# Linear attention followed by a routed mixture of experts: 64x64 score tiles, state before the scores, and a new order of the stores, gathers and first turned rows

## The chip, the cores and the metric

The kernel runs on one core of a Trainium2 chip. The metric is the device time of one execution in microseconds (us); the number shown for a kernel is the median of its runs. One execution was also taken by the hardware profiler, and all lines of a profile below come from that one execution. Engines are named as the profile names them: PE is TensorE (PEld its weight load), DVE is VectorE, ACT is ScalarE, POOL is GpSimd, SP is SyncE, which here issues nearly all plain DMAs (SPq is its queue). L573 is line 573 of the kernel.

## The reference

The input is q, k, v and f_logit of shape 4 x 8 x 768 x 48 (batch, heads, positions, head dimension), all fp32. The first part is a recurrence over the positions of each head:

```python
f = 1.0 / (1.0 + np.exp(-f_logit))
for t in range(S):
    state = f[:, :, t, :, None] * state + np.einsum('bhd,bhe->bhde', k[:, :, t], v[:, :, t])
    y[:, :, t] = np.einsum('bhd,bhde->bhe', q[:, :, t], state)
```

Its result becomes x, 3072 rows of 384. The second part routes every row to two of eight experts by noisy logits, and adds up their weighted results:

```python
noisy_logits = x @ w_gate + np.log1p(np.exp(x @ w_noise)) * noise
top2 = np.argpartition(-noisy_logits, 2, axis=1)[:, :2]      # weights: softmax over the two
h = np.maximum(x[mask] @ w1[e], 0.0)                         # w1: 384 x 1024
out[mask] += top2_w[mask, k, None] * (h @ w2[e])             # w2: 1024 x 384
```

## The kernel before

The recurrence is worked in chunks of 128 positions. There are 24 chunks, n = c * 4 + b: block c of six along the sequence, batch b of four. Each chunk covers all eight heads, two heads (a pair hp, with halves par 0 and 1 in partitions 0 to 63 and 64 to 127) side by side in 128 partitions, each head padded from 48 to 64. With L the running sum of the logarithms of the forget gates, the chunk needs P = exp(-L) and Q = exp(L); q times P is called qP and k times Q is called kQ (`scaled`). The stages of a chunk are:

- `forget` turns f on PE (fp, L533) and makes its logarithm on ACT. `summed` is a scan on DVE (L547). `decays` makes P, Q and `far`, a copy of the last column of L, on ACT (L552, L554, L555).
- `scaled` turns q and k on PE (qp and kp, L533) and multiplies them on DVE into qP and kQ (L559, L561), reading PSUM.
- `scores` turns kQ back on PE into kn (L567), where n // 4 < 5, and multiplies kQ and qP of every head, 128 x 128, into sc (L573). Eight heads fill two banks of PSUM. DVE multiplies them by the causal mask, 0 or 1, into A (L576).
- `output` adds v times A (L591) and, where c > 0, state times qP (L602) in the same banks y; between them stands ds, the product of kn and v (L597). ACT copies y out (L606) and ds out (L611); POOL makes the next state (L615, L618, L619).
- `features` multiplies y by a matrix that brings it back to rows and gives the logits of the router too (xp, L626). DVE adds the logits up (L629), ACT copies the rows, xs (L631), and a store of xs to x_rows in DRAM is put on the list xw.

A matmul's tile of the array follows from its operands: 64 contracted rows and 128 columns of the stationary operand are written 64*128 in the profile, and so on.

The loop runs over i, and a step i takes one stage each of different chunks: in steady state forget of chunk i+3, scaled of i+1, scores of i, summed of i+2, output of i-1, decays of i+2, features of i-2. A last call ties every engine's instructions to the order in which the program wrote them, so each engine's order is that of the loop, and no instruction overtakes another on its engine.

Loads are written after the stage of the same step: f after forget, q and k for three chunks ahead after scaled, v after scores. All go through SP; so do the stores of x_rows, taken from the list xw after scaled (L632), parts of the first experts' weights (L834, L837) and the clearing of `out`. Buffers of f, q, k and v are rings of 5, 4, 4 and 6 chunks.

Routing of a block c starts after its four chunks: `route` makes the entries and their slots, and POOL writes them into lists in DRAM by indirect DMA (L703, "puts", at most one in every second or third slot of the loop). When the first three blocks are routed, `first_loads` begins for the first 256 rows of experts 0 to 3: `fetch` reads a piece of the list by SP (slots, L808), `gather` reads the rows that it names by POOL's indirect DMA (xg, L819), and `turned` turns them on PE (xgp, L855) and copies them. `first_loads` is moved on by one at each slot of the loop, seven slots per step, and waits by counting slots. Its order of acts and pauses is a table of its own. Once "turned" is done, `pieces`, the products of the experts, are written between the last stages of the attention (hp, L907).

After the attention come the experts' products, from about 153 us to the end. They aren't changed.

## Time and profile before

| | |
|---|---|
| median of 3 runs | 655.39 us (652.59 to 659.07) |
| the profiled execution's own time | 659.87 us |
| its span, first to last instruction | 658.1 us |
| mean granted clock of TensorE | 0.987 |
| PE busy | 637.8 us (97%) |
| PEld, DVE busy | 551.1 us (84%), 442.8 us (67%) |
| ACT, POOL busy | 254.1 us (39%), 270.2 us (41%) |
| DMA, mean bandwidth | 145 GB/s, 96.31 MB |
| packets under 512 B | 115600 of 153897 |
| sc, L573, 384 records | 64*128, mean 291 ns |
| y, L602, 320 records | 64*64, mean 286 ns |

A record is one entry of the profile. A duration of a matmul's record includes its way through the array, so records of one engine overlap; the time that a block of matmuls costs is read from the start of its first record to the start of the next block. A group's "idle" is the time for which the engine had stood still before it, and what ended that is named behind an arrow. In the chain of waits each piece of time is put down to what the end of the execution waited for. The windows give the busy time of every engine in a stretch, then the granted clock, the share of time in which the 16 DMA engines were busy, and GB/s.

### The profile page before, as it was taken

The numbers are of one execution on the slowest core, as the hardware profiler recorded it, in microseconds if no ns is written. First come the engines' busy times: TensorE is split into PE (matmuls) and PEld (weight loads), VectorE is DVE, ScalarE is ACT, GpSimd is POOL, SyncE is SP. The second block draws the span as 40 slices with busy tenths as digits, with TensorE's granted clock in tenths as the row PEclk, the third lists the DMA queues.
The fourth block names the chain that finished last, engine by engine and source line by source line (L and its number), as shares of the span: only waits on it lengthen the run. The fifth ranks groups of instructions, "written<-read, shape, count | busy, mean of one in ns | idle before, by whom it ended". The sixth has DMA issues, their size and how long they took to land.

```text
span 658.1 us, 12894 instructions
## 1 busy us (share of the span) xinstructions
PE 637.8 (97%) x4883; PEld 551.1 (84%) x4883; DVE 442.8 (67%) x993; ACT 254.1 (39%) x602; POOL 270.2 (41%) x301
## 2 busy tenths in 40 slices
PE   8999999979999999999999999999999999999991
PEld 8999999868989999989758965995698579899891
DVE  6777877954566577677657575666666666766751
ACT  6876776642222133233332233223332332232320
POOL 7743999743188521252501450334035114413021
PEclk9999999998999999999999999999999999999996
DMA  9999898774799323368707560925275247602112
GB/s 191 193 220 205 181 191 173 179 209 110 256 348 237 64 36 86 82 192 286 195 28 245 98 192 0 316 41 176 74 242 127 63 143 191 178 2 26 21 25 29
DMA packets 153897, 96.31 MB, mean 146 GB/s; under 512 B 115600, under 2 KB 146320, under 8 KB 153824
## 3 DMA queue, kind: packets, MB, share of 16 engines
q1 hardware_dynamic: 141648, 76.12, 42.0%
q0 software_dynamic: 12176, 19.25, 15.0%
q8 instruction: 41, 0.67, 0.4%
q14 instruction: 32, 0.26, 0.1%
HBM read 75.97 MB, written 19.62 MB: 145 GB/s over the span
## 4 chain that ended last, share of the span: by engine, by line
PE 90%; DMA 5%; SPq 1%; DVE 1%; POOL 1%; issue 0%; ACT 0%; POOLq 0%; DVEq 0%
PE y L1014 31%; PE P L932 8%; PE W L932 5%; PE Z L932 5%; PE V L932 5%; PE X L932 5%; PE hp L907 5%; PE sc L573 4%; PE y L591 4%; PE xp L626 3%; PE xgp L855 2%; PE y L602 2%; PE kp L533 1%; PE ds L597 1%; PE fp L533 1%; PE qp L533 1%
## 5 line engine op out<-in xcount | busy, mean ns | idle before, releaser
L1023 POOL DMA_INDIRECT out_dram<-ys,slots x48 | 80.3, 1672 | 150.0 <-ACT ys L1084 121.9
L1014 PE MATMUL y<-qk_all,f_all 128*128 128x192 f32 x576 | 105.3, 327 | 0.5 <-DVE f_all L996 0.5
L1014 PEld LDWEIGHTS y<-qk_all,f_all 128*128 128x128 f32 x576 | 93.3, 190 | 1.1 <-DVE f_all L996 1.1
L819 POOL DMA_INDIRECT xg<-x_rows,slots x48 | 52.9, 1102 | 50.8 <-DMA slots<-lists 35.0
L1014 PE MATMUL y<-w,hs_b 128*128 128x192 f32 x320 | 59.1, 328 | 0.0
L703 POOL DMA_INDIRECT lists<-entry,sloti x48 | 54.8, 1142 | 10.3 <-issue 9.5
L1014 PEld LDWEIGHTS y<-w,hs_b 128*128 128x128 f32 x320 | 52.9, 190 | 0.9
L1158 POOL DMA_INDIRECT out_dram<-ys_q,slots_q x5 | 8.6, 1720 | 104.4 <-DVE ys_q L1156 104.4
L907 PE MATMUL hp<-xt_a,w 128*128 128x256 f32 x192 | 43.4, 382 | 0.0
L968 ACT ACTIVATE hs_b<-hs_b 128x256 f32<-128x256 f32 (+1 forms) x32 | 15.1, 470 | 71.7 <-DVE hs_b L948 71.7
L907 PEld LDWEIGHTS hp<-xt_a,w 128*128 128x128 f32 x192 | 35.9, 190 | 4.9 <-issue 0.3
L932 PE MATMUL X<-xt_a,w 128*128 128x256 f32 (+1 forms) x128 | 39.7, 432 | 0.0
L932 PE MATMUL Z<-xt_b,v_all 128*128 128x256 f32 (+1 forms) x128 | 39.7, 432 | 0.0
L1073 DVE TENSOR_TENSOR ys<-P,y 128x192 f32<-128x192 f32 x24 | 8.5, 354 | 41.6 <-PE y L1014 25.6
L948 DVE TENSOR_TENSOR hs_b<-hs_a,X 128x256 f32<-128x256 f32 (+1 forms) x32 | 15.6, 487 | 29.9 <-PE X L932 29.7
L576 DVE TENSOR_TENSOR A<-sc,causal 128x1024 f32<-128x1024 f32 x24 | 29.3, 1221 | 8.9 <-PE sc L573 8.8
L1014 PE MATMUL y<-w,f_all 128*128 128x192 f32 x192 | 35.2, 326 | 0.0
L1084 ACT ACTIVATE ys<-ys,slots 128x384 f32<-128x384 f32 x23 | 14.1, 615 | 54.1 <-DVE ys L1080 54.1
L932 PEld LDWEIGHTS X<-xt_a,w 128*128 128x128 f32 x128 | 24.3, 190 | 10.1
L932 PEld LDWEIGHTS Z<-xt_b,v_all 128*128 128x128 f32 x128 | 24.3, 190 | 10.1
L948 DVE TENSOR_TENSOR hs_a<-hs_a,P 128x256 f32<-128x256 f32 (+1 forms) x64 | 31.1, 486 | 1.4
L1014 PEld LDWEIGHTS y<-w,f_all 128*128 128x128 f32 x192 | 31.8, 190 | 0.0
(200 smaller groups left out, 1442.2 us busy)
## 6 DMA issues: line engine op xcount, KB each, us to landing
w<-in_moe_w_dram SPq DMA_DIRECT2D x16, 1536.0 KB, 8.5
w_q<-in_moe_w_dram SPq DMA_DIRECT2D x10, 1536.0 KB, 10.3
w<-in_moe_w_dram SPq DMA_DIRECT2D x16, 384.0 KB, 6.1
f_all<-in_f_logit_dram SPq DMA_DIRECT2D x24, 192.0 KB, 3.7
qk_all<-in_q_dram SPq DMA_DIRECT2D x24, 192.0 KB, 4.9
qk_all<-in_k_dram SPq DMA_DIRECT2D x24, 192.0 KB, 4.9
v_all<-in_v_dram SPq DMA_DIRECT2D x24, 192.0 KB, 4.4
x_rows<-xs SPq DMA_DIRECT2D x24, 192.0 KB, 4.4
```

Source lines behind the costliest of these rows:

```text
L533: nc.tensor.transpose(p[:, cols(hp)], flat[:, cols(hp)], ident)
L573: nc.tensor.matmul(sc[:, par, cols(hp)], lhsT=kQ[n][rows(par), cols(hp)], rhs=qP[n][rows(par), cols(hp)], start=True, stop=True)
L576: nc.vector.tensor_tensor(A[n].rearrange("j r (a i) -> j (r a) i", i=C), sc.rearrange("j r (a i) -> j (r a) i", i=C), causal.unsqueeze(1). ...
L591: nc.tensor.matmul(at(hp, par), lhsT=vt[:, 2 * hp + par, :], rhs=A[n][:, par, cols(hp)], start=(hp < 2), stop=(c == 0 and hp >= HP - 2))
L626: nc.tensor.matmul(xp[:, hp, :], lhsT=yT[n][:, hp % 2, cols(hp // 2)], rhs=w_rt[:, hp, :], start=True, stop=True)
L703: into = nc.gpsimd.indirect_dma_start(out=lists, out_offset=bass.IndirectOffsetOnAxis(ap=sloti[:, r, b:b + 1], axis=0), in_=entry[:, c, b, ...
L819: nc.gpsimd.indirect_dma_start(out=xg[p][:, s, :], out_offset=None, in_=x_rows[0:HALF * B * C] if p < NE else x_rows, in_offset=bass.Indir ...
L907: nc.tensor.matmul(hp[:, o, :], lhsT=w1[home(k)][:, i, (fo + o) * 128:(fo + o + 1) * 128], rhs=xt_a[:, i, k % 2 * 256:(k % 2 + 1) * 256], ...
L932: nc.tensor.matmul(to, lhsT=x, rhs=y, start=start, stop=stop)
L948: nc.vector.tensor_tensor(to, x, y, ALU.add)
L1014: nc.tensor.matmul(P[name], lhsT=x[:, o, :], rhs=y[:, o, :], start=(o == 0), stop=(o == FH - 1))
L1023: into = nc.gpsimd.indirect_dma_start(out=out, out_offset=bass.IndirectOffsetOnAxis(ap=slots[p][:, s, 2:3], axis=0), in_=ys[s], in_offset= ...
```

## The change

- **Scores.** The 128 x 128 scores of a head are made as 64 x 64 tiles of the array. Of the four quarters of a head (early and late keys, early and late queries), that of late keys and early queries is always zero under the mask, and isn't computed. Each head has two products: one of one half of the keys with all 128 queries, and one of the other half with the late 64 queries. PSUM for the scores (`sc_all`) is taken once and cleared once by DVE, so what is never written is zero.
- **Swapped halves.** For pairs hp 2 and 3 (heads 4 to 7) the two halves of the 128 keys are swapped in kQ, and so in kn, in the scores and in v. `scaled` therefore writes kQ by two operations; v is loaded by three DMAs, one for heads 0 to 3 and one for each half of heads 4 to 7; the mask has a plane for each pair hp.
- **State before the scores.** `from_state`, the product of state and qP, of chunk n-1 is written between kn and the scores of chunk n, and opens the accumulation in y.
- **Q and far** are made at the end of step i for chunk i+2 (`rising`), after features of that step, in place of within `decays`.
- **Stores of x_rows** are written after the stage output, so after the loads of v, in place of after scaled.
- **`first_loads`** starts two slots sooner, gathers the rows of p = 1 before the turning of p = 0, and turns p = 0 six slots after the last gather.
- **The empty list** that clears the lists has half the size and is stored twice.

```diff
@@ -422,8 +422,8 @@
         turns.append(turns.pop(0))
         return turns[-1].tile([128, 512], F32, tag="one", name=name)
 
-    def two_banks(name):
-        return ps2.tile([128, 2, 512], F32, tag="two", name=name)
+    sc_all = ps2.tile([128, 2, 512], F32, tag="two", name="sc_all")
+    nc.vector.memset(sc_all, 0.0)
 
 
     ident = const.tile([128, 128], F32, tag="ident", name="ident")
@@ -463,9 +463,12 @@
     over_of = counting("over_of", [[QS, NI]], base=3 * 256)
     block = counting("block", [[1, NI]])
 
-    causal = const.tile([128, 128], F32, tag="causal", name="causal")
-    nc.gpsimd.affine_select(out=causal, in_=ones, compare_op=ALU.is_ge, fill=0.0, base=0,
-                            pattern=[[1, 128]], channel_multiplier=-1)
+    T = C // 2
+    causal = const.tile([128, HP, 128], F32, tag="causal", name="causal")
+    for hp in range(HP):
+        for base, n in ((0, 128),) if hp < HP // 2 else ((T, 128), (-T, T)):
+            nc.gpsimd.affine_select(out=causal[0:n, hp], in_=(causal[0:n, hp] if n == T else ones), compare_op=ALU.is_ge, fill=0.0,
+                                    base=base, pattern=[[1, 128]], channel_multiplier=-1)
     earlier = const.tile([128, 128], F32, tag="earlier", name="earlier")
     nc.gpsimd.affine_select(out=earlier, in_=ones, compare_op=ALU.is_ge, fill=0.0, base=-1,
                             pattern=[[1, 128]], channel_multiplier=-1)
@@ -474,7 +477,7 @@
     LR = E * N + 256
     x_rows = tc.dram_tile([N, DM], F32, name="x_rows")
     lists = tc.dram_tile([LR, 4], U32, name="lists")
-    empty = const.tile([128, LR // 128, 4], U32, tag="empty", name="empty")
+    empty = const.tile([128, LR // 256, 4], U32, tag="empty", name="empty")
 
     cap = [const.tile([128, HP, C], F32, tag=f"cap{i}", name=f"cap{i}") for i in range(2)]
     for i in range(2):
@@ -518,8 +521,15 @@
     def load(nm, n):
         c, b = n // B, n % B
         if n < NCH * B:
-            nc.sync.dma_start(out=pads[nm][n % RING[nm]][:, :, 0:D],
-                              in_={"f": f_logit, "q": q, "k": k, "v": v}[nm][b, :, c * C:(c + 1) * C, :].rearrange("h t d -> t h d"))
+            to = pads[nm][n % RING[nm]][:, :, 0:D]
+            rows_in = {"f": f_logit, "q": q, "k": k, "v": v}[nm][b, :, c * C:(c + 1) * C, :]
+            if nm != "v":
+                nc.sync.dma_start(out=to, in_=rows_in.rearrange("h t d -> t h d"))
+                return
+            nc.sync.dma_start(out=to[:, 0:H // 2], in_=rows_in[0:H // 2].rearrange("h t d -> t h d"))
+            for half in range(2):
+                nc.sync.dma_start(out=to[half * T:(half + 1) * T, H // 2:],
+                                  in_=rows_in[H // 2:, (1 - half) * T:(2 - half) * T].rearrange("h t d -> t h d"))
 
     def clamp(n, engine=nc.gpsimd):
         if n < NCH * B:
@@ -551,14 +561,20 @@
         P[n] = wk.tile([128, HP * C], F32, tag="P", name=f"P_{n}", bufs=4)
         nc.scalar.activation(P[n], L[n], AF.Exp, scale=-1.0)
         Q[n] = wk.tile([128, HP * C], F32, tag="Q", name=f"Q_{n}")
-        nc.scalar.activation(Q[n], L[n], AF.Exp)
-        nc.scalar.copy(far[:, n, :], L[n].rearrange("d (a t) -> d a t", t=C)[:, :, C - 1])
+
+    def rising(n):
+        if 0 <= n < NS:
+            nc.scalar.activation(Q[n], L[n], AF.Exp)
+            nc.scalar.copy(far[:, n, :], L[n].rearrange("d (a t) -> d a t", t=C)[:, :, C - 1])
 
     def scaled(n):
         qP[n] = wk.tile([128, HP * C], F32, tag="qP", name=f"qP_{n}", bufs=3)
         nc.vector.tensor_tensor(qP[n], transposed("q", n), P[n], ALU.mult)
         kQ[n] = wk.tile([128, HP * C], F32, tag="kQ", name=f"kQ_{n}")
-        nc.vector.tensor_tensor(kQ[n], transposed("k", n), Q[n], ALU.mult)
+        kt = transposed("k", n)
+        for far_ in range(2):
+            out_, x, y = (z.rearrange("d (o a s t) -> d o a s t", o=2, s=2, t=T)[:, far_] for z in (kQ[n], kt, Q[n]))
+            nc.vector.tensor_tensor(out_[:, :, ::-1, :] if far_ else out_, x, y, ALU.mult)
 
     def scores(n):
         if n // B < NCH - 1:
@@ -567,40 +583,49 @@
                 nc.tensor.transpose(kp[:, cols(hp)], kQ[n][:, cols(hp)], ident)
             kn[n] = wk.tile([C, H, DP], F32, tag="kn", name=f"kn_{n}")
             nc.scalar.copy(kn[n].rearrange("t h d -> t (h d)"), kp)
-        sc = two_banks(f"sc_{n}")
-        for hp in range(HP):
-            for par in range(2):
-                nc.tensor.matmul(sc[:, par, cols(hp)], lhsT=kQ[n][rows(par), cols(hp)],
-                                 rhs=qP[n][rows(par), cols(hp)], start=True, stop=True)
+        if n:
+            from_state(n - 1)
+        for hp in (0, 2, 1, 3):
+            for late_rows in range(2):
+                half = hp // 2 ^ late_rows
+                for par in range(2):
+                    nc.tensor.matmul(sc_all[half * T:(half + 1) * T, par, hp * C + late_rows * T:(hp + 1) * C],
+                                     lhsT=kQ[n][rows(par), hp * C + half * T:hp * C + (half + 1) * T],
+                                     rhs=qP[n][rows(par), hp * C + late_rows * T:(hp + 1) * C], start=True, stop=True)
         A[n] = wk.tile([C, 2, HP * C], F32, tag="A", name=f"A_{n}")
-        nc.vector.tensor_tensor(A[n].rearrange("j r (a i) -> j (r a) i", i=C), sc.rearrange("j r (a i) -> j (r a) i", i=C),
-                                causal.unsqueeze(1).broadcast_to((C, H, C)), ALU.mult)
+        nc.vector.tensor_tensor(A[n], sc_all, causal.rearrange("j a i -> j (a i)").unsqueeze(1).broadcast_to((C, 2, HP * C)), ALU.mult)
+
+    y_of = {}
+
+    def place(n, hp, par):
+        return y_of[n][hp % 2][rows(par ^ hp % 2), cols(hp // 2)]
+
+    def from_state(n):
+        y_of[n] = [one_bank(f"y{odd}_{n}") for odd in range(2)]
+        if n // B:
+            for hp in range(HP):
+                for par in range(2):
+                    nc.tensor.matmul(place(n, hp, par), lhsT=state[n % B][rows(par), hp, :],
+                                     rhs=qP[n][rows(par), cols(hp)], start=(hp < 2), stop=False)
 
     def output(n):
         c, b = n // B, n % B
         vt = pads["v"][n % RING["v"]]
 
 
-        y = [one_bank(f"y{odd}_{n}") for odd in range(2)]
-
-        def at(hp, par):
-            return y[hp % 2][rows(par ^ hp % 2), cols(hp // 2)]
-
+        if n not in y_of:
+            from_state(n)
+        y = y_of[n]
         for hp in range(HP):
             for par in range(2):
-                nc.tensor.matmul(at(hp, par), lhsT=vt[:, 2 * hp + par, :], rhs=A[n][:, par, cols(hp)],
-                                 start=(hp < 2), stop=(c == 0 and hp >= HP - 2))
+                nc.tensor.matmul(place(n, hp, par), lhsT=vt[:, 2 * hp + par, :], rhs=A[n][:, par, cols(hp)],
+                                 start=(c == 0 and hp < 2), stop=(hp >= HP - 2))
         if c < NCH - 1:
             ds = one_bank(f"ds_{n}")
             for hp in range(HP):
                 for par in range(2):
                     nc.tensor.matmul(ds[rows(par), hp * DP:(hp + 1) * DP], lhsT=kn[n][:, 2 * hp + par, :],
                                      rhs=vt[:, 2 * hp + par, :], start=True, stop=True)
-        if c:
-            for hp in range(HP):
-                for par in range(2):
-                    nc.tensor.matmul(at(hp, par), lhsT=state[b][rows(par), hp, :],
-                                     rhs=qP[n][rows(par), cols(hp)], start=False, stop=(hp >= HP - 2))
         yT[n] = wk.tile([128, 2, HP // 2 * C], F32, tag="yT", name=f"yT_{n}")
         for odd in range(2):
             nc.scalar.copy(yT[n][:, odd, :], y[odd][:, 0:HP // 2 * C])
@@ -1258,10 +1283,10 @@
     def first_loads():
         while n_routed < HALF or len(n_put) < HALF * B * 2:
             yield
-        for _ in range(7):
+        for _ in range(5):
             yield
-        for what, p, pause in (("fetch", 1, 4), ("first", 0, 0), ("second", 0, 3), ("fetch", 2, 7), ("turned", 0, 0),
-                               ("first", 1, 3), ("second", 1, 1), ("fetch", 3, 1)):
+        for what, p, pause in (("fetch", 1, 4), ("first", 0, 0), ("second", 0, 3), ("fetch", 2, 5), ("first", 1, 1), ("second", 1, 6),
+                               ("turned", 0, 0), ("fetch", 3, 1)):
             if what == "fetch":
                 ahead(what, p)
             elif what == "first":
@@ -1311,16 +1336,17 @@
                         load(nm, n + 3)
                 if n in (1, 2):
                     load_router(n - 1)
-                while xw:
-                    xw.pop(0)()
             elif stage is scores:
                 for m in (n + 1,) if n < 4 else (2 * n - 3, 2 * n - 2) if n < 6 else (n + 3,):
                     load("v", m)
                 if n in (2, 6, 7, 8, 9, 10):
                     load_router(2 + (2, 6, 7, 8, 9, 10).index(n))
                 elif n == 5:
-                    nc.sync.dma_start(out=lists.rearrange("(p r) w -> p r w", p=128), in_=empty)
+                    for part in range(2):
+                        nc.sync.dma_start(out=lists.rearrange("(g p r) w -> g p r w", g=2, p=128)[part], in_=empty)
             elif stage is output:
+                while xw:
+                    xw.pop(0)()
                 if 9 <= n < 17:
                     part_of_weights(0, 1 + (n - 9) // 4, (n - 9) % 4)
                 elif n >= NS - 2:
@@ -1336,6 +1362,7 @@
             if done["turned"] and (n_first < 5 or i >= NS - 3 and stage is not forget) and (n_first < 11 or i >= NS - 1):
                 next(pieces)
                 n_first += 1
+        rising(i + 2)
         if i < 0:
             warm_up(4)
         if i >= NS - 1:
```

## The prediction

> **What bounds the kernel now.** I read the windows, then the order of instructions in one chunk, the chain of waits around 140 us, and SyncE's queue.
>
> Windows (busy us of PE, PEld, DVE, ACT and POOL, granted clock, DMA share, GB/s):
>
> ```profile
> 60.00:100.00 40.00, 40.00 (x592) 36.44 (x595) 32.41 (x83) 29.08 (x79) 33.15 (x46) 1.00 0.88 185
> ...
> 126.00:132.00 6.00, 6.00 (x88) 5.33 (x87) 5.86 (x13) 3.69 (x10) 2.38 (x4) 1.00 0.80 173
> ...
> 142.00:146.00 4.00, 0.00 (x0) 0.00 (x0) 0.71 (x4) 0.48 (x1) 3.26 (x6) 0.93 0.89 276
> 146.00:153.00 7.00, 6.88 (x56) 5.49 (x57) 3.77 (x10) 0.34 (x2) 5.72 (x9) 0.55 0.55 100
> ```
>
> TensorE sets the pace of the attention phase, but by 126 VectorE has 0.14 us free in 6. Then TensorE stands still and goes on at half clock: 0.55.
>
> The order of one chunk (start, duration):
>
> ```profile
> 102.77 0.60 PE L567 MATMUL kp<-ident,kQ 128*128 128x128 f32 x4
> 103.30 1.16 PE L573 MATMUL sc<-qP,kQ 64*128 64x128 f32 x16
> ...
> 104.95 1.09 PE L591 MATMUL y<-A,v_all 128*64 128x128 f32 x16
> 105.88 0.63 PE L597 MATMUL ds<-v_all,kn 128*64 128x64 f32 x16
> 106.44 0.67 PE L602 MATMUL y<-qP,st 64*64 64x128 f32 x16
> 107.04 1.15 PE L626 MATMUL xp<-w_rt,yT 128*128 128x112 f32 x8
> ```
>
> Starts matter here, since durations overlap: 1.09 from the start of the scores to the next block's, 0.60 for state. From chunk 4 to 19 a chunk takes 6.00 (the starts of xp in the trace: 45.52, 51.52, 57.52), a little more where routing's small products stand between. The array's shape changes four times in these lines and once more back to 128*128: 64*128, 128*64, 64*64, 128*128.
>
> The stall, from TensorE's order of time and from the chain:
>
> ```profile
> 140.82 1.15 PE L626 MATMUL xp<-w_rt,yT 128*128 128x112 f32 x8
> 146.12 0.87 PE L855 MATMUL xgp<-ident,xg 128*128 128x128 f32 x3 [4.16 <-DMA xg<-x_rows,slots]
> 146.93 2.08 PE L573 MATMUL sc<-qP,kQ 64*128 64x128 f32 x16
> 148.94 0.90 PE L855 MATMUL xgp<-ident,xg 128*128 128x128 f32 x3
> 149.77 1.98 PE L591 MATMUL y<-A,v_all 128*64 128x128 f32 x16
> ```
> ```profile
> 134.87 4.37 DMA slots<-lists
> ...
> 140.06 5.93 DMA xg<-x_rows,slots
> ```
>
> SyncE's queue, where a duration above some 0.4 us means that an issue was held up:
>
> ```profile
> 123.87 1.24 SPq L521 DMA_DIRECT2D qk_all<-in_k_dram  x1
> 125.20 3.56 SPq L632 DMA_DIRECT2D x_rows<-xs  x1
> ...
> 130.10 1.92 SPq L521 DMA_DIRECT2D qk_all<-in_k_dram  x1
> ```
>
> From the start to 136 us SyncE is always inside an issue, about 0.1 apart. It isn't waiting for the data: every x_rows store is issued 4 us or more after its xs is written. It is held up by transfers in flight. k of chunk 22 was issued at 123.87 and landed 8.46 later, at 132.3; TensorE takes it at 132.9.
>
> **What the Trainium skill says.** "TensorEngine Tiling (Array Packing)", Key Properties: changing the tiling mode drains TensorE; Available Configurations: 64x64 gives four independent tiles. The trace agrees: sixteen records of state in 64*64 take 0.60, sixteen of as many columns in 64*128 or 128*64 take 1.09 and 0.93. "TensorE: Matmul & The Clock Gate", What's actually happening: after an idle window of about 3.4 us the clock is halved. The trace agrees: 4.16 idle, then scores at 2.08 against 1.16. [...]
>
> **The change, part by part.**
>
> *TensorE, scores.* Each product is two records[...]. Before, eight products of 128 columns lie on two tiles: eight records on each, at about 107 ns by the starts of their pairs, 855. After, sixteen products lie on four tiles; each tile has two of 128 columns and two of 64, so four records of each. State starts four records of 128 columns every 109 ns, ds a pair of 64 columns every 58.5: 4 x 109 + 4 x 58.5 = 670, -185 a chunk. If only two tiles worked at a time it would be twice that, 1340, +485. I take -185, since state's records show four.
>
> *TensorE, order.* State moves ahead of the scores, so both use one shape. Differences between a block's span and its steady rate give the switches: kn to sc 194, sc to y 142, ds to state 151, state to xp 201, together 690. After: kn to state 144 (93 at the end of kn, 51 at the start of state, from the same differences), none to scores, sc to y 142, ds to xp 187 (as it stands at c = 0, where no state is), together 473: -215. At c = 0 no state exists, and only some -50 of it.
>
> Per chunk -235 for c = 0 (4 chunks) and -400 after (20 chunks): -0.9 - 8.0 = -8.9 us. Bounds: -10, and with the scores at 1340, 4 x 0.435 + 20 x 0.27 = +7.1.
>
> *VectorE.* kQ becomes two operations of 256 columns. From 512 columns at 681 ns and 192 at 354, 256 cost about 420: +160 a chunk, 3.8 in all. Before 119 us it has room. From 119 to 138 it has 0.2 in 6, so there it, not TensorE, sets the pace: three chunks keep about 6.0. A keeps its 1.22: one mask of full width instead of a broadcast, 0. The clearing of sc_all is about one A, 1.2, before ones and the pads; VectorE had 0.6 free before the first clamp, so at most +0.6 at the start.
>
> *GpSimd.* Five more mask instructions at 0.28 are 1.4, in a gap of 3.72 ahead of its first clamp: 0. Halving the empty table halves its four clears (0.53 each). If that cover were gone, 1.4 would delay the third f.
>
> *ScalarE.* Q and far move behind xs. xs leaves about 0.8 (0.63 + 0.19) sooner; Q that much later. It has over 1 us free a chunk: 0, bounds -0.3 and +0.5, as VectorE's kQ waits for Q.
>
> *SyncE.* v of a chunk takes three issues instead of one: 48 more, at least 0.42 + 0.05 each, with the same bytes in pieces of 192 B. Two more are +0.94 a chunk. In 123 to 132 six issues took 8.7, of which 6 x 0.47 = 2.8 is issuing; the rest is held-up time, and the new issues lie in that. I take 0; bounds 0 and +0.94. Halving the store of the empty lists adds one issue, 0. Storing x_rows after v leaves the loads of q and k where they were, relative to everything but v.
>
> *The tail.* The fetch of slots goes ahead of v of chunk 23, and behind one x_rows instead of two: about -1 to -2. Then slots land near 138, the gather (0.8 later, 5.9 long) near 144.5. Ahead of the first xgp now stand state of 22, scores of 23, A products of 22 and xp of 21: 0.6 + 0.95 + 0.95 + 1.0, about 3.3 us more work. The gap of 4.16 shrinks to 0.3 or so, below the idle window, and the half clock goes with it: scores 2.08 - 1.16, y 1.98 - 1.09, two xgp 0.38 each, state 0.27 and a little, 3.1. Together -7.0. Late next: w2 of expert 1, whose loads cost TensorE 1.2 at 190 us, unchanged.
>
> **What limits the first gain.** k of chunk 19 is issued by 107.0 and used at 115.1; landing takes 4.4 or more. TensorE would come 4 x 0.235 + 15 x 0.4 = 6.9 sooner, at 108.2, and wait until 111.4: some 3.2. k of chunk 22 leaves spare time of 132.9 - 132.3 = 0.6, chunk 23 about 1.2. The transfers were saturated without TensorE's help, so their dates stay. So of 8.9 about 1.5 remains up to chunk 23 and after it: -1.5. Sum: -1.5 - 7.0 + 0.3 (start) = -8.2. The profiled execution took 659.87, so it would be 651.7; it stands 4.5 above the median, so I forecast 655.4 - 8.2 = **647.2**. Own range 643.5 to 650.5.
>
> **Rivals.**
>
> - *The transfers follow TensorE after all*: DMA share is only 0.72 to 0.88 after 60 us, so perhaps the issues hold each other up and pass sooner with new order. Then -8.9 stays, less 1 for VectorE from 119 to 138: -7.9 - 7.0 + 0.3 = -14.6, 640.8. Against: a full queue at every chunk.
> - *The stall stays*: the gather is bound to the slots fetch, this to SyncE's queue; if the v issues ahead of it take the gain and SyncE comes there 1.5 later, xg lands at 147 and the gap is some 3 us: -1.5 - 1.2, with most of the half clock still there: 652.7.
> - *Slower: the v issues throttle the loads.* By the program each SyncE transfer reuses one of eight landing signals, and waits for the one before on it; with v in three, eight transfers are one chunk instead of 1.3. Where landings reach 7 to 8.5 us against a cycle of 7.1, an issue waits for a landing. If the cycle grows by the full 0.94 from chunk 9 to 23, k of 23 comes 14 late: +14 - 1 spare - 7 = +6: 661. It decides from 8.2 / 15 = 0.55 us a chunk on. Against: the transfer six back had landed 0.3 to 4.5 before each issue ended.
> - *The tiles run two at a time* (the scores don't do what their shape says): +7.1 in place of -8.9, with the stall gone since TensorE comes later: 655.4 + 7.1 - 7.0 = 655.5. Against: the state records.
>
> **How the numbers follow.** Forecast 0.50, full gain 0.14, stall stays 0.15, two tiles 0.06, slower 0.15. A measurement of this kernel can tell about 1% (6.5 us) from no change. Faster by over 1% (below 648.8): 0.72 of the forecast's 0.50, all of the full gain, 0.03 of the third: 0.53. Slower by over 1% (above 661.9): 0.08 of the slower case's 0.15 and 0.02 of two tiles: 0.10. The rest, 0.37. The range runs from the full gain to below the slower case's middle: 639.5 to 658.
>
> **What would show it.** Right: scores at 0.67 plus one switch of some 0.14 and state directly ahead of them; chunk periods of 5.6 up to chunk 18; waits for k or q of 1 to 3 us from chunk 19 on; no idle of 3 us at the first xgp and no half clock at 145 to 152; end of attention 8 us sooner. Wrong: landings of k that move by more than 2 us either way, scores above 1.1, a new idle time of over 3.4 us from chunk 18 on with half clock, or xgp still waiting 4 us for the gather.

## The result, and the profile after

The changed kernel is slower: 673.33 us median (669.97 to 674.53) against 653.99 for the kernel before (651.47 to 659.07) on the same chip, ratio on record 1.0263, 95% interval 1.0206 to 1.0319 (the quotient of the two medians is a little higher, 1.030). The forecast was 647.2, the range 639.5 to 658. The experiments below ran on several chips, on which the kernel before takes 662 to 673 us, so only ratios to the kernel before on the same chip are compared. Some executions fall into a slower state, over 1.5% longer, as two of the four of `a_noswap_of` below did.

The profiled execution took 673.62, its span is 671.8. The first expert product (hp) starts at 169.3, against 152.5 before: +16.8. From there to the end it is 502.5 against 505.6: -3.1. But hp isn't the same place in the two: before, three blocks of xp, one of y<-A and one of state still stand behind it, after the change one of xp, and that alone is some 3.4 us. Farther on, where TensorE's order is the same again, the difference is steady: the turned rows xgp that start at 260.74 before start at 273.13 after, and TensorE stays 12.4 us late up to its last product. The loss lies ahead of that, then, in the attention phase. Its windows (busy us of PE, PEld, DVE, ACT and POOL, granted clock, DMA share, GB/s):

```profile
20.00:60.00 40.00, 38.35 (x684) 35.77 (x681) 30.91 (x65) 32.01 (x84) 19.73 (x29) 1.00 0.83 168
60.00:100.00 40.00, 33.60 (x559) 30.39 (x560) 28.57 (x67) 24.20 (x63) 26.90 (x37) 0.99 0.79 158
100.00:142.00 42.00, 38.23 (x611) 35.23 (x604) 29.13 (x82) 26.43 (x72) 29.13 (x42) 0.89 0.83 174
```

TensorE had stood full in each of these before; now it is idle for 1.7, 6.4 and 3.8 us and part of the rest runs at a lower clock. The DMA engines are busy for a smaller share in the first of them: 0.83 from 20 to 60 us, where it had been 0.99. This is the first window before:

```profile
20.00:60.00 40.00, 40.00 (x569) 36.84 (x567) 30.18 (x61) 31.90 (x84) 19.09 (x28) 1.00 0.99 210
```

A chunk in which nothing waits does what the forecast said (TensorE in order of time):

```profile
128.12 1.15 PE L651 MATMUL xp<-w_rt,yT 128*128 128x112 f32 x8
...
130.94 0.68 PE L608 MATMUL y<-qP,st 64*64 64x128 f32 x16
131.43 0.86 PE L592 MATMUL sc_all<-qP,kQ 64*64 64x128 f32 x32
132.22 1.09 PE L621 MATMUL y<-A,v_all 128*64 128x128 f32 x16
...
133.71 1.15 PE L651 MATMUL xp<-w_rt,yT 128*128 128x112 f32 x8
```

5.59 us from xp to xp, in place of 6.00; state and scores take 1.28 together, where they had taken 1.69. But few chunks are like that. The chain of waits (start, duration, what) shows why:

```profile
102.34 4.27 DMA x_rows<-xs
106.68 0.48 ACT xs L656
107.16 0.53 ACT Q L567
...
110.51 4.81 DMA x_rows<-xs
115.39 0.49 ACT xs L656
115.93 0.55 PE y L608 x10
```

There are three buffers of xs. The copy of chunk 12 at 106.68 starts as the store of chunk 9 lands (102.34 + 4.27). That store was issued at 102.34, although its xs had been copied at 82.88: SyncE came to it only then. Q now stands behind xs on ScalarE, and so do the following copies. ScalarE in order of time, after:

```profile
104.50 0.63 ACT L562 ACTIVATE P<-L 128x512 f32<-128x512 f32 x1 [0.19 <-DVE sp L676]
106.68 0.48 ACT L656 COPY xs<-xp 128x384 f32<-128x384 f32 x1 [1.55 <-DMA x_rows<-xs]
107.06 0.63 ACT L567 ACTIVATE Q<-L 128x512 f32<-128x512 f32 x1
```

The longest waits up to 200 us (total, times, longest):

```profile
ACT xs L656 <- DMA x_rows<-xs: 21.9, 10, 4.4
...
DVE kQ L577 <- ACT Q L567: 18.3, 13, 4.4
```

and TensorE's own:

```profile
PE y L608 <- ACT xs L656: 9.0, 9, 2.0
PE kp L543 <- DMA qk_all<-in_k_dram: 3.0, 4, 1.3
PE xgp L880 <- DMA xg<-x_rows,slots: 2.7, 2, 1.9
```

The waits for xs cost more than their length, since the half clock follows some of them (TensorE in order of time; y<-A takes 1.09 at full clock):

```profile
115.93 0.55 PE L608 MATMUL y<-qP,st 64*64 64x128 f32 x10 [2.04 <-ACT xs L656]
...
118.77 1.98 PE L621 MATMUL y<-A,v_all 128*64 128x128 f32 x16
```

The granted clock is 0.50 from 99.4 to 102.8, from 116.5 to 123.3 and from 147.2 to 150.6, together 13.6 us where it had been 6.8 before. The idle times at these places are 1.93, 2.04 and 1.79 us.

In the list of TensorE's waits, the last line is the old stall at the first turned rows: 2.7 in two pieces, and no half clock shows behind them. The long stall is gone, so that part of the change did work. SyncE's queue, in the same stretch:

```profile
96.76 3.36 SPq L527 DMA_DIRECT2D qk_all<-in_k_dram  x1
100.17 0.75 SPq L529 DMA_DIRECT2D v_all<-in_v_dram  x1
100.97 1.27 SPq L531 DMA_DIRECT2D v_all<-in_v_dram  x2
102.34 0.55 SPq L657 DMA_DIRECT2D x_rows<-xs  x1
```

Three issues of v take 2.1 us ahead of the store, and yet the issue of k is held for 3.36. From one x_rows to the next it is 8.1 us here (94.29, 102.34, 110.51).

### The profile page after: what moved, and what is told of

Its sections match the earlier page's. It is cut to its first block, busy times and chain, and to the rows that moved or that the text cites. A ratio compares the mean times of both kernels' runs of the same rounds, so it can differ in the third digit from the quotient of the medians.

```text
span 671.8 us, 13762 instructions
## 1 busy us (share of the span) xinstructions
PE 636.4 (95%) x5267; PEld 552.2 (82%) x5267; DVE 448.4 (67%) x1018; ACT 255.5 (38%) x602; POOL 269.9 (40%) x306
## 4 chain that ended last, share of the span: by engine, by line
PE 78%; DMA 9%; ACT 5%; DVE 2%; SPq 2%; POOL 2%; issue 1%; POOLq 0%; ACTq 0%; DVEq 0%
PE y L1039 32%; PE P L957 8%; PE hp L932 6%; DMA x_rows<-xs 6%; PE W L957 5%; PE Z L957 5%; PE V L957 5%; PE X L957 5%; PE xgp L880 2%; PE xp L651 1%; PE y L621 1%; DMA xg<-x_rows,slots 1%; PE yp_q L1177 1%; PE hp_q L1162 1%; SPq L527 1%
## 5 line engine op out<-in xcount | busy, mean ns | idle before, releaser
L728 POOL DMA_INDIRECT lists<-entry,sloti x48 | 52.0, 1083 | 10.5 <-issue 9.5
L537 POOL TENSOR_SCALAR f_all<-f_all 128x384 f32<-128x384 f32 x22 | 26.4, 1204 | 23.3 <-DMA f_all<-in_f_logit_dram 15.4
L596 DVE TENSOR_TENSOR A<-sc_all,causal 128x1024 f32<-128x1024 f32 x24 | 29.3, 1221 | 6.7 <-PE sc_all L592 6.0
```

The lines of the kernel that those rows point to most:

```text
L537: engine.tensor_scalar(raw, raw, XMIN, None, ALU.max)
L596: nc.vector.tensor_tensor(A[n], sc_all, causal.rearrange("j a i -> j (a i)").unsqueeze(1).broadcast_to((C, 2, HP * C)), ALU.mult)
L728: into = nc.gpsimd.indirect_dma_start(out=lists, out_offset=bass.IndirectOffsetOnAxis(ap=sloti[:, r, b:b + 1], axis=0), in_=entry[:, c, b, ...
```

## The experiments

**Which part costs it.** Theory A was the loop just shown: a store of x_rows that is late holds the buffer of xs, and with it the copy to xs three chunks on and Q behind that. Theory B was the loads of v in three: SyncE comes too late to everything. Four runs on one chip:

`b_vsplit`: the kernel before, with only v in three loads, halves in natural order.

```diff
+            nc.sync.dma_start(out=to[:, 0:H // 2], in_=rows_in[0:H // 2].rearrange("h t d -> t h d"))
+            for half in range(2):
+                nc.sync.dma_start(out=to[half * T:(half + 1) * T, H // 2:],
+                                  in_=rows_in[H // 2:, half * T:(half + 1) * T].rearrange("h t d -> t h d"))
```

> The kernel before with only the loads of v in three DMAs, halves in natural order. Theory A (the loop through the three xs buffers: a store of x_rows issued late holds the next copy of xs on ACT, and with it Q and TensorE): x_rows still stands ahead of v and Q ahead of xs, so 654 to 658. Theory B (the three issues of v slow SyncE's queue, 0.6 us for each half of heads 4 to 7): a chunk of loads takes 1.2 us longer, k of chunk 23 comes 10 to 15 us late: 662 to 668.

Measured: ratio 1.011 (1.0024 to 1.0196). The DMA share from 20 to 60 us is 0.83, as in the changed kernel.

`a_xs5`: `bufs=3` of xs becomes `bufs=5` in the changed kernel.

> The changed kernel with five buffers of xs in place of three. Theory A: the waits of xs for x_rows (21.9 us up to 200 us) vanish, and the time falls to 655 to 660. Theory B: TensorE then waits for k and q in place of xs; 668 to 673.

Measured: 1.0194 (1.0095 to 1.0293). The waits of xs for x_rows are gone from the list; TensorE's longest are now these:

```profile
PE qp L543 <- DMA qk_all<-in_q_dram: 5.8, 4, 1.9
PE qp L543 <- ACT f L549: 3.3, 1, 3.3
PE kp L543 <- DMA qk_all<-in_k_dram: 3.1, 5, 1.3
```

Beside these TensorE waits 5.7 us for nothing that the profile shows (see `b_first` below). With the loop cut, the loads come too late in its place: theory B's picture.

`a_xback`: in the changed kernel, the two lines `while xw: xw.pop(0)()` move from the stage output back to the stage scaled.

> The changed kernel with the stores of x_rows back after scaled, ahead of the loads of v. Theory A: the store is issued some 3 us sooner, most of the xs waits go: 656 to 662. Theory B: 668 to 673, since the same issues stand in the queue.

Measured: 1.0107 (1.0021 to 1.0192).

`a_qback`: in the changed kernel, Q and far return into `decays`, and `rising(i + 2)` goes.

> The changed kernel with Q and far back in decays, ahead of xs on ACT. Theory A: xs still waits for x_rows, but kQ no longer waits behind it; y's copies still do: 662 to 669. Theory B: 670 to 674, no change.

Measured: 1.019 (1.0103 to 1.0276). These intervals of almost 1% each way can't rank the four, nor place them against the changed kernel, which wasn't among them. The next four ran with it, on another chip.

`after_again`: the changed kernel itself.

> The changed kernel once more, beside the three that follow: a ratio of 1.02 to 1.03 to the kernel before, as measured first.

Measured: 1.0244 (1.0179 to 1.0308).

`b_vheads`: the kernel before with v in three loads of all 128 partitions.

```diff
+            nc.sync.dma_start(out=to[:, 0:H // 2], in_=rows_in[0:H // 2].rearrange("h t d -> t h d"))
+            for a in range(H // 2, H, 2):
+                nc.sync.dma_start(out=to[:, a:a + 2], in_=rows_in[a:a + 2].rearrange("h t d -> t h d"))
```

> The kernel before with v in three loads, all of 128 partitions (heads 0 to 3, 4 and 5, 6 and 7). Theory B1 (the number of issues is what slows SyncE's queue): as with the halves, 1.01 of the kernel before, DMA share near 0.83 from 20 to 60 us. Theory B2 (loads of 64 partitions are what is slow, 0.60 us of issuing each against 0.42): within 0.4% of the kernel before, DMA share above 0.93.

Measured: 1.0214 (1.0156 to 1.0271), DMA share 0.88. So nothing but the number of loads of v, in the kernel before, costs 2%. Whole loads of 128 partitions don't help. TensorE's waits of this run:

```profile
PE xgp L861 <- DMA xg<-x_rows,slots: 6.7, 1, 6.7
PE kp L539 <- DMA qk_all<-in_k_dram: 6.3, 4, 2.0
```

k comes late, and with the old order of the first rows the stall grows from 4.2 to 6.7 us. The stores come late as well, and hold xs (ScalarE's wait, up to 190 us), though they stand ahead of v here:

```profile
ACT xs L637 <- DMA x_rows<-xs: 12.7, 8, 3.5
```

In the profile before there is no such wait. So the loop doesn't need the new order of the stores; a late SyncE is enough. TensorE itself waits little for xs here (0.4).

`a_noswap`: the changed kernel without the swap.

```diff
-            nc.sync.dma_start(out=to[:, 0:H // 2], in_=rows_in[0:H // 2].rearrange("h t d -> t h d"))
...
+            nc.sync.dma_start(out=to, in_=rows_in.rearrange("h t d -> t h d"))
-        for far_ in range(2):
...
+        nc.vector.tensor_tensor(kQ[n], transposed("k", n), Q[n], ALU.mult)
-                half = hp // 2 ^ late_rows
+                half = late_rows
```

> The changed kernel without the swapped halves: v in one load, kQ in one operation, scores with early keys in the tiles of columns 0 to 63 for all heads (872 ns by the steady rates in place of 670). Theory B (the three issues of v): the DMA share of 20 to 60 us returns to 0.95 or more and the time falls by 8 us or more against the changed kernel, to within 1% of the kernel before. Theory A alone (the loop through the xs buffers): x_rows is still stored after v, so it falls by 3 us at most.

Measured: 0.9942 (0.9921 to 0.9962), DMA share 0.98. With v in one load, the rest of the change is faster than the kernel before, although the stores of x_rows still stand behind v and Q behind xs. Against the changed kernel on the same chip that is 3.0% by the two ratios, and 17 us by the medians (658.27 and 675.22). This run also takes back the two operations of kQ and the mask of the swap; what these cost by themselves wasn't run, but `b_vheads` has neither, and is slow.

`a_noswap_xq`: the same, with x_rows and Q back as in `a_xback` and `a_qback`.

> The same with the stores of x_rows back after scaled, and Q and far back in decays: of the change there remain the state ahead of the scores, the cleared sc_all, the order of the first rows and the split empty list. Theory A adds to B: another 3 to 6 us less than with the swap alone undone, so 0.985 to 0.995 of the kernel before, since the stall at the first turned rows is gone (7 us). Theory B alone: the same time as with only the swap undone.

Measured: 0.9927 (0.9894 to 0.9959): no difference that can be told. With v in one load the new order of the stores and of Q costs next to nothing. The loop closes in both, for a few chunks: xs waits for landings for 8.5 us in `a_noswap` and for 7.7 here.

`a_xq`: the changed kernel with x_rows and Q both back, v still in three.

> The changed kernel with both the stores of x_rows after scaled and Q and far in decays; v still in three loads. If the three issues alone cost what was measured with the loads of v undone: 1.018 to 1.026 of the kernel before, hardly below the changed kernel. If the waits of xs for x_rows, with Q behind, cost half of it: 1.005 to 1.013.

Measured: 1.0135 (1.0091 to 1.018), on a third chip. Two of its waits, up to 190 us:

```profile
ACT xs L653 <- DMA x_rows<-xs: 19.6, 9, 4.0
...
PE kp L543 <- DMA qk_all<-in_k_dram: 10.7, 7, 4.0
```

So even the old order of both doesn't open the loop: xs waits almost as long as in the changed kernel (21.9). What went is Q's place behind it, and TensorE's own wait for xs fell from 9.0 to 2.0, while that for k rose from 3.0 to 10.7. The sums: 0.9942 for the rest of the change and about 2.1% for three loads of v (`b_vheads`) make 1.015, close to `a_xq`; the new order of the stores and of Q would then be the 1.1% from there to the changed kernel (1.0244). But the shares aren't shown. With the 1.1% of `b_vsplit`, whose loads have the shape of the changed kernel's, the first sum is 1.005, and 0.9% stay over; the interval of `b_vsplit`, 1.0024 to 1.0196, is wide enough for either. What is shown is this: the three loads alone make the kernel before slower, and the rest of the change without them is no slower than the kernel before. The new order of the stores and of Q seems to cost something only beside the three loads (1.0135 and 1.0244, on two chips, with intervals that just touch). Theory B is what starts it; theory A is at work in its wake, and its share stays open.

**What is short on SyncE's queue.** `b_tiny`: the kernel before, two DMAs of 16 bytes more after each load of v.

```diff
+            if nm == "v":
+                for i in range(2):
+                    nc.sync.dma_start(out=bits[0:1, n, i], in_=v[b, 0:1, c * C + i, 0:4])
```

> The kernel before with two more DMAs on SyncE's queue after each load of v, 16 bytes each, into a tile that nothing reads. Theory B3 (each DMA on the queue has a price of its own, whatever it carries): 1.01 to 1.02 of the kernel before, DMA share of 20 to 60 us below 0.9. Theory B4 (it is the data of v in pieces that lands later, or the smaller pieces that leave fewer bytes in flight): within 0.4%.

Measured: 1.005 (1.0021 to 1.008), DMA share 0.94. A tiny issue takes 0.29 us of the queue (median), some 0.8 a chunk for two with the gaps. That is some 19 us for all 48, and the time rose by 3.4: most of the added time was taken in somewhere, as the prediction had it for v, but not all.

`b_spload`: no DMA more, but SyncE reads the batch number from SBUF ahead of each load of q, k and v.

```diff
+                at = nc.values_load(batch[0:1, b:b + 1], engines=[mybir.EngineType.SP], min_val=0, max_val=B - 1, ...)
+                rows_in = from_[bass.ds(at, 1)][:, :, c * C:(c + 1) * C, :].rearrange("o h t d -> t (o h) d")
```

> The kernel before with no more DMAs, but SyncE reads the batch number of each q and k load, and of each v load, from SBUF into a register first (0.28 us and some 0.15 beside, three times a chunk from chunk 4 on, about 1.3 us of SyncE's time a chunk). Theory C (SyncE's own time for issuing is the bound): 1.01 to 1.02 of the kernel before. Theory D (what is short is not SyncE's time but what a DMA holds while in flight, as one of the eight landing signals): within 0.4%.

Measured: 1.0127 (1.0085 to 1.0169). SyncE's queue in it:

```profile
85.96 1.18 SPq L532 DMA_DIRECT2D f_all<-in_f_logit_dram  x1
87.71 1.38 SPq L532 DMA_DIRECT2D qk_all<-in_q_dram  x1
89.66 3.97 SPq L532 DMA_DIRECT2D qk_all<-in_k_dram  x1
```

Between issues there is 0.57 (87.14 to 87.71) in place of 0.1, and still the load of k is held for 3.97. So SyncE's own time counts, even where the queue is held up beside it: the held time doesn't take all of the added time in. Sixty readings of 0.47 are some 28 us of the queue, and the time rose by 8.5. The DMA share from 20 to 60 us stayed at 0.96, though, so this isn't the whole of what three loads of v do.

`a_actx`: the changed kernel, the store of x_rows issued by ScalarE (`nc.scalar.dma_start` for `nc.sync.dma_start`).

> The changed kernel with the stores of x_rows issued by ACT's queue, right where they stand. If SyncE's time is what the three issues of v take up, one issue fewer there (0.6 us a chunk at least) gives back half: 1.005 to 1.015 of the kernel before. If the transfers themselves are the limit: no change, 1.02 to 1.03, or worse, since ACT is then held up in its issues.

Measured: 1.0248 (1.0211 to 1.0285), no gain. It doesn't settle the question, since ScalarE's queue now waits itself: this line is from its waits up to 190 us.

```profile
ACT P L562 <- DMA qk_all<-in_q_dram: 12.3, 2, 7.1
```

P needs no q. By the program, loads on SyncE and stores on ScalarE take the same eight landing signals in turn, so the store ahead of P has to wait for the load that had its signal last. `c_actx`, the same move in the kernel without the swap (with the clear of sc_all as in `c_late0` below):

> The same with the stores of x_rows issued by ACT. If SyncE's time holds the loads of chunks 10 to 23: 4 to 6 us less than with the clear moved alone, 0.983 to 0.987 of the kernel before. If the transfers hold them: the same, or more by the time that ACT stands in the issues (0.4 to 0.6 us a chunk).

Measured: 1.0115 (1.0041 to 1.0189), against 0.991 for `c_late0` on the same chip: worse, in the same way.

The landing signals, the mechanism of the prediction's slower rival, can be tried on the changed kernel itself. Its chunks have eight transfers on SyncE's queue, so the load of k reuses the signal of the load of k one chunk before. TensorE and SyncE in order of time:

```profile
96.20 0.63 PE L543 MATMUL kp<-ident,qk_all 128*128 128x128 f32 x4 [1.31 <-DMA qk_all<-in_k_dram]
```
```profile
88.13 3.01 SPq L527 DMA_DIRECT2D qk_all<-in_k_dram  x1
...
96.76 3.36 SPq L527 DMA_DIRECT2D qk_all<-in_k_dram  x1
```

The k issued at 88.13 was in by 96.20, since TensorE began on it then. The next one begins at 96.76 and is still held for 3.36. So in this chunk it isn't the signal that holds it. Nor is it the buffer: there are four of k, the load at 96.76 is that of chunk 16, and TensorE turned the k of chunk 12 at 74.75.

**The other parts, and a version that beats both.** `b_first`: the kernel before with the new counts and the new table of `first_loads`, nothing else.

> The kernel before with the new order of the first rows alone. By the prediction the idle 4.16 us before the first turned rows and the half clock after it go: 0.987 to 0.992 of the kernel before. If the gather only waits for the same fetch: 0.998 to 1.002.

Measured: 0.9946 (0.9924 to 0.9967): half of the forecast gain. The wait for xg is gone, but another came at the same place (TensorE in order of time):

```profile
148.83 0.45 PE L602 MATMUL y<-qP,st 64*64 64x128 f32 x3 [1.11 <-issue]
150.26 0.45 PE L602 MATMUL y<-qP,st 64*64 64x128 f32 x4 [0.98 <-issue]
...
157.76 0.85 PE L855 MATMUL xgp<-ident,xg 128*128 128x128 f32 x3
158.53 1.98 PE L591 MATMUL y<-A,v_all 128*64 128x128 f32 x16
```

TensorE does a few records, waits about 1 us for nothing that the profile shows, does a few more; 5.2 us in all, and the half clock comes with it (y at 1.98). This can't be put down to the new order, though. Between 20 and 180 us all eight profiles from this chip and from that of the first four runs have such waits (2.2 to 7.4 us), with the old order of the first rows (`b_vsplit`, `b_tiny`, `b_spload`, `a_noswap_of`) as with the new one; the twelve profiles from other chips, of either order, have none. On the two chips that have them the kernel before takes 670 and 673 us, on the others 654 to 663. So these waits go with the chip, and what the new order brings on a chip without them was not run by itself.

`a_noswap_of`: `a_noswap_xq` with the old order of the first rows.

> The changed kernel without the swap, with the stores of x_rows, Q and the order of the first rows as before: what remains are the state ahead of the scores and the scores in 64x64 tiles. If transfers hold most of what TensorE saves: 0.996 to 1.002 of the kernel before; if TensorE's saving counts in full (0.2 us a chunk, 4 to 5 in all): 0.992 to 0.994.

Measured: 1.0147 (1.0058 to 1.0236) on record, but that takes in two executions of 684.02 and 685.62 us. The other two, 672.98 and 674.43, are only 0.4 to 0.6% above the 670.43 of the kernel before. In its profile, one of these two, TensorE waits 4.6 us for xs and 5.0 for nothing that the profile shows, most of the latter between 150 and 162. It ran on the same chip as `b_first`. Two executions are too few to price the old order of the first rows.

`c_late0`: `a_noswap`, with sc_all cleared after the pads of v.

```diff
-    nc.vector.memset(sc_all, 0.0)
...
     clamp(1, nc.vector)
     pad("v")
+    nc.vector.memset(sc_all, 0.0)
```

> The changed kernel without the swap, sc_all cleared after the pads of v and the first two clamps in place of ahead of ones. The first turning of f starts 1.1 to 1.3 us sooner. If the start is on the path: 0.991 to 0.993 of the kernel before (0.994 without it); if the loads set the first chunks anyway: 0.994.

Measured: 0.991 (0.9879 to 0.9942). TensorE's first work waits for `ones` 1.1 us, as before the change, and not 2.2. But the first turning of f starts only 0.3 us sooner than in `a_noswap` (4.67 and 4.97), not the 1.1 to 1.3 expected. The gain of about 0.3% over `a_noswap` lies within the intervals.

`c_xq`: `c_late0` with x_rows and Q back as before.

> The changed kernel without the swap, with sc_all cleared later, and with the stores of x_rows and Q and far where they were before: what remains of the change is state ahead of the scores, 64x64 score tiles, the cleared sc_all and the order of the first rows. If each of these parts adds: 0.988 to 0.991 of the kernel before.

Measured: 0.9942 (0.9917 to 0.9967), a little less good than expected, and no better than `a_noswap_xq` (0.9927), which has the clear at its early place: the place of the clear can't be told.

`c_few`: the same with the router's noise in one load.

```diff
+            nc.sync.dma_start(out=noise.rearrange("p b c e -> p (b c) e"), in_=moe_noise.rearrange("(g p) e -> p g e", p=C))
-                if n in (2, 6, 7, 8, 9, 10):
+                if n == 2:
```

> The same with the noise of the router in one load in place of six, of the same pieces of 32 bytes: five issues fewer on SyncE's queue by chunk 10. If each issue costs the queue its 0.6 us, all later loads stand 3 us sooner and TensorE gains up to 3 us: 0.984 to 0.988 of the kernel before. If the transfers set the dates: as without it.

Measured: 0.9913 (0.9884 to 0.9941), 655.39 us beside 662.15 for the kernel before on this chip. The sign is that of a price of each issue, the size (0.3% against `c_xq`) is within the intervals. `c_late0` and `c_few` are the best of the runs, 0.9% below the kernel before, with `a_noswap_xq` and `a_noswap` within the intervals of both.

## Why the prediction was wrong, point by point

- **TensorE, scores and order.** Right. 5.59 us a chunk against a forecast of 5.6, four tiles at a time (0.79 for the scores with the switch behind them). The rival of two tiles falls.
- **SyncE.** This is the step that failed: "the rest is held-up time, and the new issues lie in that. I take 0". The lines showed SyncE inside an issue without a break, and I read the time above 0.42 as slack that an issue more could fill. But on a queue that never stands idle, what the held time doesn't take in moves every date behind it. The term that I put at 0 measured 2.1% in `b_vheads` and 1.1% in `b_vsplit`, 14 and 7 us; `b_spload` showed that time alone on this engine has a price, with no transfer added. What holds the issues, transfers in flight as I wrote or something else, no run shows. One line of the reading was wrong too: not every store of x_rows was issued 4 us or more after its xs was written. For chunks 5 to 8 it was 2.1 to 3.3; the xs were written by then all the same. The rival "the v issues throttle the loads" had the direction and the place, and was given 0.15 and 661. It lacked the loop, and its mechanism, the eight signals, isn't what held the one issue that could be tried.
- **x_rows after v.** "Storing x_rows after v leaves the loads of q and k where they were" was weighed for the loads alone. A store also frees a buffer: xs has three, and the copy three chunks on waits for the landing. In the profile before, the store of chunk 15 landed at 132.5 and xs of chunk 18 began at 134.2, a margin of 1.7 us, the smallest of all, which could have been read. In the changed kernel that margin is gone for most chunks. `a_xq` against the changed kernel gives about 1.1% for this and Q together, across two chips.
- **ScalarE.** "It has over 1 us free a chunk: 0" holds for its work, not for its order. With xs held, Q behind it is held too: 18.3 us of waits of kQ. With v in one load, kQ still waits 8.0 us in `a_noswap`, and this costs nothing measurable (beside `a_noswap_xq`).
- **VectorE.** Each half of kQ took 418 ns against an estimate of 420. The clear took 0.91 (1.2 estimated). The first turning of f came 1.3 us late (4.03 to 5.32), where I had allowed 0.6. Only 0.4 of that is the line of VectorE's work behind the clear: the first clamp of f, which PE turns next, began at 3.94 in place of 3.52. The clamp itself then took 1.23 in place of 0.36, and ended 0.2 after GpSimd was done with the masks and `cap` (4.95). In `c_late0`, with fewer masks and the clear out of the way, it took 0.94. So GpSimd's longer mask work, which I put at 0, is the likelier cause of the rest; no run takes it away alone.
- **The clock.** The prediction went by an idle window of about 3.4 us, and looked for half clock only behind one. In the changed kernel no idle time from 20 to 150 us was longer than 2.04, and the half clock came all the same, three times. Not every such idle time brings it: 1.97 us in `a_noswap` brought none. From 20 to 200 us half clock was 17 us in `after_again`, and none in `a_noswap` and `a_noswap_xq`, so it is a part of what the late loads and stores cost, which the prediction's sums for a slower case lack.
- **The tail.** The idle time before the first turned rows went from 4.16 in one piece to 2.7 in two, without half clock there, though everything around it came later. The order of the first rows alone brought 0.5%, not the 7 us (1.1%), on a chip on which waits that the profile can't name stand at the same place with either order. What it brings elsewhere stays open.
- **What limits the first gain.** That the loads would keep much of TensorE's saving back fits. Without the three loads, state order, tiles and first rows together brought 0.6 to 0.9%, some 4 to 6 us, where the forecast had 8.2 and the full gain 14.6. A part of the difference is the swap, which is gone there: without it the scores block took 0.98 in place of 0.78, so TensorE saved some 0.2 us a chunk and not 0.4.
- What stays open: what holds an issue on SyncE's queue while the DMA engines are busy for only 0.83 of the time, how the loss divides between the three loads and the new order of the stores and of Q, and what TensorE waits for on the two chips with waits that the profile doesn't name.

## What to carry to other kernels

An engine that is never idle may be a bound, even if its instructions look held up by others. Don't put an issue added to it at nothing: of the added time, about a fifth came through for the tiny issues, a third for the readings, and a quarter to a half for the loads of v (`b_vsplit`, `b_vheads`). Look at who stands behind it. Before a store is moved later, find the buffer that it frees and the margin until that buffer is written again; before an instruction is moved behind another on an in-order engine, ask what that other one can wait for. A DMA that is cut into pieces for the sake of another engine is paid for on the queue. And before a wait is put down to a change, see whether the same wait stands in profiles of other versions from the same chip.

## What the runs showed of the hardware that was not expected

- The same bytes of v in three loads in place of one lowered the DMA engines' share from 0.99 to 0.83 (halves) and 0.88 (by heads) from 20 to 60 us, while SyncE was inside an issue all the time.
- Issuing a load of 64 partitions with four heads took at least 0.60 us (48 KB, changed kernel), of 128 partitions with two heads at least 0.42 (`b_vheads`, 48 KB too), of 128 partitions with eight heads at least 0.37 to 0.42 (192 KB), of 16 bytes at least 0.23 (`b_tiny`). So the issue of a load did not get shorter with its bytes.
- TensorE can stand for 1 us at a time, every few records, with nothing in the profile that it waits for: 5.2 us in `b_first`, and 2.2 to 7.4 in all eight profiles from two of the chips, none in the twelve from the others.
- The clock was halved behind idle times of TensorE of 1.8 to 2.0 us (changed kernel, 3.4 to 6.8 us at 0.50), and in `b_first` behind three of 1.0 to 1.1 with few records between them (10.2 us at 0.50).
- A clamp of 128x384 on VectorE took 0.36 us in the kernel before and 1.23 in the changed one, where GpSimd was writing masks and `cap` at the time.
